# Sharing the normal forms of a LayerNorm between ScalarE and VectorE in an FFT mixer and MLP training step

## The chip, the cores and the metric

One core of a Trainium2 chip runs the whole step as one program. The metric is the device time of that program in microseconds (us); for the kernel before, it is the median of three runs. Engines are named as the profile names them: PE (TensorE's matmuls), PEld (its weight loads), DVE (VectorE), ACT (ScalarE), POOL (GpSimd) and SP (SyncE, which here only issues DMAs).

## The reference

The reference computes a forward pass and all gradients of two residual blocks over x of shape 2048 x 448 (bf16). Cut to what matters:

```python
def _layernorm(x, axis=-1, eps=1e-5):
    m = jnp.mean(x, axis=axis, keepdims=True)
    v = jnp.var(x, axis=axis, keepdims=True)
    return (x - m) / jnp.sqrt(v + eps)

def _A_ref(x, w_r, w_i):                   # spectral mixer
    X = jnp.fft.rfft2(x.astype(jnp.float32), axes=(-2, -1))
    y = jnp.fft.irfft2(X * (w_r + 1j * w_i), s=(S, D), axes=(-2, -1))
    return y.astype(jnp.bfloat16)

def _B_ref(x, w1, b1, w2, b2):             # token MLP, with a second layernorm inside
    u = gelu(jnp.einsum("bsd,sf->bdf", _layernorm(x), w1) + b1)
    return (jnp.einsum("bdf,fs->bds", u, w2) + b2).transpose(0, 2, 1)

h  = x + _A_ref(_layernorm(x), A_w_r, A_w_i)
h2 = h + _B_ref(_layernorm(h), B_w1, B_b1, B_w2, B_b2)
# outputs: h2 and the gradients of x, w_r, w_i, w1, b1, w2, b2 for a given grad_out
```

## The kernel before

The 2048 rows of x are held as 16 tiles of 128 partitions (row q * 16 + h in partition q of tile h), and the tiles are worked in four row groups g of four tiles. The stages around the change are these, in the order of the code.

**Statistics and normal forms** (class `Norm`). For each tile DVE computes bn_stats and bn_aggr (L279, L281). After the fourth tile of a group, `finish` runs: ACT takes the square root (L289), DVE the reciprocal and two small products (L290 to L293), and then ACT writes four normal forms, one per tile, as scale and bias from columns (L296). The class is used twice: for x (tiles `xln`) and later for h (tiles `hln`).

**Step 1 of the FFT** (`fft_rows`). For one row group DVE folds the normal forms into even and odd parts (`eo`, L303 to L305); PE runs 16 small matmuls into four PSUM tiles (L311); each PSUM tile is evicted into `zt` by ACT (L194) or DVE (L196), as a string of four letters says ("a" or "v"). In the forward pass it runs once per group right behind the statistics of that group.

**dg.** The product of grad_out and w2, needed much later, is cut into 14 pieces dg(j) of 16 matmuls (L438), each on one transposed tile of w2 (`w2T`, four buffers, loaded by DMA transposes on SP at L175). dg(0) to dg(3) stand behind step 1 in the code, each of dg(1) to dg(4) may start only behind the L311 matmuls of one row group (`folded[...][0]`), and the rest stand behind the whole spectral chain.

**The spectral chain.** `fft_cols` (step 2: L329 to L343, then output matmuls L321 to L323 with the table `hf`), the complex product `cmul` (L362 to L365), `ifft_cols` (L379 to L400), `ifft_rows` (L409 to L418), and for each of the 16 row tiles of the result the sum with x (L475) and h's statistics. The third part of the table `hf` is the negative of the second, made by DVE (L199, called at L458) behind a given instruction of group 3's step 1: `folded[3][1]`, the last instruction of the fold.

**The MLP.** 14 accumulations over the 16 `hln` tiles (L519, w1 in tiles `w1c` that take over the space of `zt` and others), gelu and its derivative, the second product (L587), then the backward pass, which calls `fft_rows`, `fft_cols` and the inverse steps once more with other tables.

The order of each engine's instructions is written when the program is built, by a scheduler that works with estimated durations and lets work that comes earlier in the code go first where several instructions could start. So PE's order is not the code's order: dg's matmuls appear in the trace between the steps of the spectral chain. Loads given to `nxt` are issued by SP in the order of the code, one behind the other. `issue_after` adds an order between two instructions of the same engine.

Of the kernel before, what the change touches and what calls it, by code (L numbers as in the profile page):

```python
# [13 lines left out]
ALU = mybir.AluOpType  # L14
ACT = mybir.ActivationFunctionType
# [98 lines left out]
def kernel(  # L114
# [21 lines left out]
    ve, ac, po, pe = nc.vector, nc.scalar, nc.gpsimd, nc.tensor  # L136
# [7 lines left out]
    def slot(i, shape, name):  # L144
        return big.tile(shape, BF16, tag=f"s{i}", name=name)
# [4 lines left out]
    def e4(shape, name):  # L150
        return ring.tile(shape, BF16, tag="e4", bufs=3, name=name)
# [7 lines left out]
    def col(n, name, dtype=F32):  # L159
        return ring.tile([P, n], dtype, tag=name, bufs=4, name=name)  # L160
# [4 lines left out]
    def ps_sp(shape, dtype=F32):  # L165
        return psum.tile(shape, dtype, tag="sp", bufs=5, name="ps_sp")
# [24 lines left out]

    def ev(out, in_, on):
        if on == "a":
            ac.copy(out=out, in_=in_)  # L194
        else:
            ve.tensor_copy(out=out, in_=in_)  # L196

    def neg(out, in_):
        ve.tensor_scalar(out=out, in0=in_, scalar1=-1.0, scalar2=None, op0=ALU.mult)  # L199
# [5 lines left out]
    x = slot(0, [P, NT, D], "x")  # L205
# [64 lines left out]
    class Norm:  # L270
# [14 lines left out]
        def finish(self, g):  # L285
            mv = self.mv[:, :].rearrange("p (i c) -> p i c", c=2)
            r = self.rstd[:, 4 * g:4 * g + 4]
            sq = col(4, f"sq_{self.nm}")
            ac.activation(out=sq[:], in_=mv[:, :, 1], func=ACT.Sqrt, bias=self.eps_col[:], scale=self.scale)  # L289
            ve.reciprocal(out=r, in_=sq[:])  # L290
            ve.tensor_scalar(out=self.rneg[:, 4 * g:4 * g + 4], in0=r, scalar1=self.back, scalar2=None, op0=ALU.mult)
            nb = col(4, f"nb_{self.nm}")
            ve.scalar_tensor_tensor(out=nb[:], in0=mv[:, :, 0], scalar=-1.0, in1=r, op0=ALU.mult, op1=ALU.mult)  # L293
            for i in range(4):
                h = 4 * g + i
                ac.activation(out=self.dst[:, h, :], in_=self.src[:, h, :], func=ACT.Identity,  # L296
                              scale=self.rstd[:, h:h + 1], bias=nb[:, i:i + 1])


    def fft_rows(src, zt, g, on, behind=None):  # L300
        eo = e4([P, 4, D], "eo")
        a, b = src[:, 4 * g:4 * g + 4, 1:224], src[:, 4 * g:4 * g + 4, 447:224:-1]
        ve.tensor_tensor(out=eo[:, :, 1:224], in0=a, in1=b, op=ALU.add)  # L303
        ve.tensor_tensor(out=eo[:, :, 225:448], in0=a, in1=b, op=ALU.subtract)
        fold = ve.tensor_copy(out=eo[:, :, 0:225:224], in_=src[:, 4 * g:4 * g + 4, 0:225:224])  # L305
        for i in range(4):
            h = 4 * g + i
            pz = ps_sp([P, 4, P])
            with tc.issue_after(behind.ins) if behind is not None else nullcontext():
                for c, o in enumerate((0, 97, 225, 320)):  # L310
                    last = pe.matmul(pz[:, c, :], lhsT=eo[:, i, o:o + P], rhs=kf[:], start=True, stop=True)  # L311
            ev(zt[:, :, :, 8 * h:8 * h + 8], pz[:, :, :].rearrange("p c (s k) -> p c s k", k=8), on[i])
        return last, fold

    def fft_cols(zt, dtab, dst):
        e_t = dtab[:, 0:2 * DF].rearrange("p (c k) -> p c k", c=2)
# [54 lines left out]
    def ifft_cols(ys, ab):  # L371
# [16 lines left out]
        for r in (1, 2, 3, 4, 5, 6, 7, 0, 8):  # L388
            p0 = half(r)
            if r in (0, 8):  # L390
                for kind in range(2):
                    ev(ab[:, kind, :, :, r, :], view(p0)[:, kind], "av"[kind])
                continue
            p1 = half(16 - r)
            t1 = f2([P, 2, 2, P], "t1")
            ac.copy(out=t1[:], in_=p1[:])
            st_ = 16 - 2 * r
            ve.tensor_tensor(out=ab[:, 0, :, :, r:17 - r:st_, :].rearrange("p c h k l -> p k c h l"),
                             in0=view(p0), in1=view(t1), op=ALU.add)
            ve.tensor_tensor(out=ab[:, 1, :, :, 16 - r:r - 1:-st_, :].rearrange(  # L400
                "p c h k l -> p k c h l"), in0=view(p0), in1=view(t1), op=ALU.subtract)
        return lasts[-1]

    def ifft_rows(ab, itab, h):
        a_t = itab[:, 0:2 * DF].rearrange("p (c k) -> p c k", c=2)
        b_t = itab[:, 2 * DF:4 * DF].rearrange("p (c k) -> p c k", c=2)
        pq = ps_sp([P, 2 * DF])
        for c in range(2):
            pe.matmul(pq[:, 0:DF], lhsT=ab[:, 0, c, h, :, :], rhs=a_t[:, c, :], start=(c == 0), stop=(c == 1))  # L409
        for c in range(2):  # L410
            pe.matmul(pq[:, DF:], lhsT=ab[:, 1, c, h, :, :], rhs=b_t[:, c, :], start=(c == 0), stop=(c == 1))  # L411
        eo = k1([P, 2 * DF], "eo2")
        ev(eo[:], pq[:], "a")
        py = ps_sp([P, D])
        pe.matmul(py[:, 0:DF], lhsT=kinv[:, 0, :], rhs=eo[:, 0:DF], start=True, stop=False)
        pe.matmul(py[:, DF:D], lhsT=kinv[:, 0, :], rhs=eo[:, 223:0:-1], start=False, stop=False)
        pe.matmul(py[:, 0:DF], lhsT=kinv[:, 1, :], rhs=eo[:, DF:2 * DF], start=False, stop=False)
        pe.matmul(py[:, DF:D], lhsT=kinv[:, 2, :], rhs=eo[:, DF + 223:DF:-1], start=False, stop=True)  # L418
        return py


    xln = slot(1, [P, NT, D], "xln")
    nx = Norm(x, xln, rstd_x, rneg_x, eps_x, 1.0, -1.0 / D, "x")
    zt = slot(2, [P, 4, NR, P], "zt")
    folded = []
    for g in range(4):
        for i in range(4):
            nx.stats(4 * g + i)
        folded.append(fft_rows(xln, zt, g, "avav" if g else "aava"))


    du = slot(7, [P, NFB, 450], "du")
# [148 lines left out]
    for t0 in range(0, NT, 4):  # L581
# [7 lines left out]
        for i in range(4):  # L589
# [3 lines left out]
                                    op0=ALU.add, op1=ALU.add)  # L593
# [32 lines left out]
    for h in range(NT):  # L626

        if h in (10, 14):
            fft_rows(dh, zt2, h // 4 - 2, "aava", w1_last)
        if h == 4:  # L630
            goT = slot(4, [P, 4, S], "goT")
            with tc.issue_after(w1T_last.ins):
                ld_t4(goT[:], grad_out[0])
        if h == 4:
            with tc.issue_after(w1T_last.ins):
                ld(df0[:], hnd["df0"].ap())
                ld(di1[:], hnd["di1"].ap())
        w1T = w4([P, NFB, P], "w1T")
        with tc.issue_after(chain[-1].ins):
            w1T_last = ld_t(w1T[:], w1Tv[h])  # L640
        pd = ps_mm([P, D + 1])
        for j in range(NFB):
            w1_last = pe.matmul(pd[:], lhsT=w1T[:, j, :], rhs=du[:, j, 0:D + 1], start=(j == 0), stop=(j == NFB - 1))  # L643
        norm_back(pd, True, hln[:, h, :], rstd_h[:, h:h + 1], rneg_h[:, h:h + 1], go_r[:, h, :], dh[:, h, :])


    with tc.issue_after(w1T_last.ins):
        load_w(w_b, lambda load, out, in_: load(out, in_))
    fft_rows(dh, zt2, 2, "aava")

    g_t = slot(0, [P, 4, F], "g_t")
# [119 lines left out]
```

## Time and profile before

| | |
|---|---|
| median of three runs | 372.22 us (370.95 to 372.51) |
| the profiled execution | 371.55 us |
| its span, first to last instruction | 369.8 us |
| granted TensorE clock | 1.00 |
| DMA over the span | 86.48 MB, mean 234 GB/s |

A page of the profile gives busy times per engine, the span in 40 slices, the DMA queues, the chain of work that ended last, and groups of like instructions. A timeline row reads: start, duration, engine, line, operation, tile written <- tiles read, shapes, count, and in brackets the idle time of the engine before it with what ended that. A group row reads: busy time, mean ns of one | idle time before and what ended it. A row of stretches gives, for each engine, busy us and the number of instructions, then the granted clock, the mean busy share of the DMA engines and GB/s.

### The profile page before, as it was taken

The numbers are of one execution on the slowest core, as the hardware profiler recorded it, in microseconds if no ns is written. First come the engines' busy times: TensorE is split into PE (matmuls) and PEld (weight loads), VectorE is DVE, ScalarE is ACT, GpSimd is POOL, SyncE is SP. The second block draws the span as 40 slices with busy tenths as digits, with TensorE's granted clock in tenths as the row PEclk, the third lists the DMA queues.
The fourth block names the chain that finished last, engine by engine and source line by source line (L and its number), as shares of the span: only waits on it lengthen the run. The fifth ranks groups of instructions, "written<-read, shape, count | busy, mean of one in ns | idle before, by whom it ended". The sixth has DMA issues, their size and how long they took to land.

```text
span 369.8 us, 5755 instructions
## 1 busy us (share of the span) xinstructions
PE 346.6 (94%) x2100; PEld 200.4 (54%) x2115; DVE 236.3 (64%) x557; ACT 217.4 (59%) x415; POOL 61.2 (17%) x107
## 2 busy tenths in 40 slices
PE   0698999999989999999999999999999999999996
PEld 0355667666645555555555555566655555665553
DVE  4873679967744999621167778468996566599000
ACT  2776555446659998109222234967656666777664
POOL 1000000001112211500540000101012522255311
PEclk9999999999999999999999999999999999999999
DMA  7999998997889999999998875791874444956633
GB/s 279 258 257 307 270 274 245 310 240 259 249 251 176 338 346 291 380 401 215 261 224 159 185 147 208 162 182 61 204 199 184 163 177 166 337 187 255 250 150 149
DMA packets 132524, 86.48 MB, mean 234 GB/s; under 512 B 91952, under 2 KB 123824, under 8 KB 131984
## 3 DMA queue, kind: packets, MB, share of 16 engines
q1 hardware_dynamic: 124304, 55.78, 61.2%
q0 software_dynamic: 8048, 30.31, 22.3%
q8 instruction: 16, 0.26, 0.3%
q14 instruction: 12, 0.10, 0.1%
q10 hardware_dynamic: 144, 0.03, 0.0%
HBM read 32.81 MB, written 30.76 MB: 172 GB/s over the span
## 4 chain that ended last, share of the span: by engine, by line
PE 65%; DVE 17%; ACT 8%; DMA 4%; SPq 3%; issue 2%; ACTq 0%; DVEq 0%
PE ps_mm L732 12%; PE ps_mm L662 10%; PE ps_sp L587 7%; PE ps_mm L438 6%; PE ps_mm L519 6%; PE ps_sp L519 5%; PE ps_mm L587 4%; DMA w2T<-in_B_w_dram 4%; DVE junk L615 3%; DVE junk L617 3%; ACT v L610 3%; SPq L175 2%; DVE t_r L362 2%; DVE gg L349 2%; DVE t_i L363 2%
## 5 line engine op out<-in xcount | busy, mean ns | idle before, releaser
L194 ACT CAST s<-ps_mm 128x512 bf16<-128x512 f32 (+1 forms) x107 | 57.5, 557 | 25.6 <-PE ps_mm L662 11.1
L662 PE MATMUL ps_mm<-goT,g_t 128*128 128x512 bf16 x214 | 53.3, 379 | 2.0 <-ACT s L194 1.5
L438 PE MATMUL ps_mm<-go_nat,w2T 128*128 128x448 bf16 x224 | 50.5, 357 | 1.0 <-DMA w2T<-in_B_w_dram 1.0
L732 PE MATMUL ps_mm<-du_t,hlnT 128*128 128x512 bf16 (+1 forms) x251 | 49.3, 352 | 0.3
L643 PE MATMUL ps_mm<-du,w1T 128*128 128x449 bf16 x224 | 43.4, 353 | 0.0
L732 PEld LDWEIGHTS <-hlnT 128*128 128x128 bf16 x256 | 25.1, 98 | 22.2
L587 PE MATMUL ps_sp<-gT,w2c 128*128 128x448 bf16 x140 | 35.6, 352 | 0.0
L610 ACT ACTIVATE v<-ps_mm,nm,rstd_h 128x448 f32<-128x448 f32 x16 | 11.6, 723 | 39.2 <-DVE nm L608 39.2
L172 POOL DMA_DIRECT2D out_dram<-s x29 | 15.6, 539 | 112.4 <-ACT s L194 86.3
L519 PEld LDWEIGHTS <-w1c 128*128 128x128 bf16 x224 | 21.8, 98 | 20.7 <-issue 1.9
L587 PEld LDWEIGHTS <-w2c 128*128 128x128 bf16 x224 | 21.9, 98 | 20.5
L643 PEld LDWEIGHTS <-w1T 128*128 128x128 bf16 x224 | 21.7, 97 | 20.7
L662 PEld LDWEIGHTS <-g_t 128*128 128x128 bf16 x224 | 21.6, 97 | 20.7 <-issue 1.4
L438 PEld LDWEIGHTS <-w2T 128*128 128x128 bf16 x224 | 21.9, 99 | 16.2 <-DMA w2T<-in_B_w_dram 1.9
L349 DVE TENSOR_TENSOR gg<-ps_sp,gi 128x450 bf16<-128x450 f32 x28 | 16.2, 621 | 17.0 <-ACT gi L346 17.0
L587 PE MATMUL ps_mm<-gT,w2c 128*128 128x448 bf16 x84 | 25.0, 352 | 0.0
L519 PE MATMUL ps_mm<-hln,w1c 128*128 128x448 bf16 x112 | 24.4, 352 | 0.5 <-DVE b1col L508 0.2
L194 ACT CAST eo<-ps_sp 128x450 bf16<-128x450 f32 x32 | 17.2, 538 | 12.5 <-PE ps_sp L411 12.2
L519 PE MATMUL ps_sp<-hln,w1c 128*128 128x448 bf16 x112 | 23.1, 352 | 0.0
L311 PE MATMUL ps_sp<-kf,eo 128*128 128x128 bf16 x128 | 9.3, 231 | 14.0 <-DVE eo L305 14.0
L592 DVE SCALAR_TENSOR_TENSOR h<-ps_sp,b2col,hr 128x448 bf16<-128x448 f32 x10 | 6.3, 679 | 25.1 <-PE ps_sp L587 25.1
L615 DVE CUSTOM_DVE_ANT_0 junk<-ps_sp,xr,rneg_x 128x448 bf16<-128x448 f32 x16 | 10.9, 683 | 16.3 <-ACT v L612 16.3
(146 smaller groups left out, 625.9 us busy)
## 6 DMA issues: line engine op xcount, KB each, us to landing
w1c<-in_B_w_dram SPq DMA_DIRECT2D x7, 1024.0 KB, 7.4
w2c<-in_B_w_dram SPq DMA_DIRECT2D x8, 896.0 KB, 12.6
out_dram<-s POOLq DMA_DIRECT2D x14, 512.0 KB, 2.9
out_dram<-s POOLq DMA_DIRECT2D x15, 448.0 KB, 2.9
xs_d<-xs SPq DMA_DIRECT2D x1, 1800.0 KB, 7.7
xs_b<-xs_d SPq DMA_DIRECT2D x1, 1800.0 KB, 8.9
x<-in_A_x_dram SPq DMA_DIRECT2D x4, 448.0 KB, 4.3
go_nat<-in_grad_out_dram SPq DMA_DIRECT2D x2, 896.0 KB, 7.5
```

Of the source, the lines that this page charges most:

```text
L172: return (eng or po).dma_start(out=out, in_=in_)
L194: ac.copy(out=out, in_=in_)
L349: ve.tensor_tensor(out=gg[:], in0=pr[:], in1=gi[:], op=op)
L438: pe.matmul(pg[:], lhsT=w2T[j][:, t, :], rhs=go_nat[:, t, :], start=(t == 0), stop=(t == NT - 1))
L519: pe.matmul(pu[:], lhsT=wc[:, h, o:o + P], rhs=hln[:, h, :], start=(h == 0), stop=(h == NT - 1))
L587: pe.matmul(p2[i][:], lhsT=w2c[t0 // 4][:, j, i * P:(i + 1) * P], rhs=gT[:, j, :], start=(j == 0), stop=(j == NFB - 1))
L610: ac.activation(out=v[:], in_=ps[:, 0:D], func=ACT.Identity, scale=rstd_c, bias=nm1[:])
L615: ve.tensor_tensor_reduce(out=junk[:], in0=ps[:, 0:D], in1=xhat, scale=rneg_c, scalar=0.0, op0=ALU.mult, op1=ALU.add, accum_out=nm2[:])
L617: ve.scalar_tensor_tensor(out=junk[:], in0=xhat, scalar=nm2[:], in1=v[:], op0=ALU.mult, op1=ALU.add)
L643: w1_last = pe.matmul(pd[:], lhsT=w1T[:, j, :], rhs=du[:, j, 0:D + 1], start=(j == 0), stop=(j == NFB - 1))
L662: mm = pe.matmul(pw[:], lhsT=g_t[:, c, j * P:(j + 1) * P], rhs=goT[:, c, 512 * n:512 * n + 512], start=(c == 0), stop=(c == 3))
L732: pe.matmul(pw[:, 0:wdt], lhsT=hlnT[:, c, h * P:(h + 1) * P], rhs=du_t[:, c, 512 * n:512 * n + wdt], start=(c == 0), stop=(c == 3))
```

## The change

Three things are changed. In `finish`, two of the four normal forms of a group (i = 2 and 3) are made by DVE as one tensor_scalar with two column operands, for all four groups of x and for the last group of h; the others stay on ACT. In x's step 1 the evictions of groups 0 to 2 all go to ACT ("aaaa"), while group 3 keeps "avav"; before, it was "aava" for group 0 and "avav" for the others. And `fft_rows` returns its last eviction in place of the last instruction of the fold, so that hf's negative stands behind the last eviction of group 3, which is DVE's.

```diff
     def ev(out, in_, on):
         if on == "a":
-            ac.copy(out=out, in_=in_)
-        else:
-            ve.tensor_copy(out=out, in_=in_)
+            return ac.copy(out=out, in_=in_)
+        return ve.tensor_copy(out=out, in_=in_)
...
             for i in range(4):
                 h = 4 * g + i
-                ac.activation(out=self.dst[:, h, :], in_=self.src[:, h, :], func=ACT.Identity,
-                              scale=self.rstd[:, h:h + 1], bias=nb[:, i:i + 1])
+
+                if i > 1 and (self.nm == "x" or g == 3):
+                    ve.tensor_scalar(out=self.dst[:, h, :], in0=self.src[:, h, :], scalar1=self.rstd[:, h:h + 1],
+                                     scalar2=nb[:, i:i + 1], op0=ALU.mult, op1=ALU.add)
+                else:
+                    ac.activation(out=self.dst[:, h, :], in_=self.src[:, h, :], func=ACT.Identity,
+                                  scale=self.rstd[:, h:h + 1], bias=nb[:, i:i + 1])
...
-        fold = ve.tensor_copy(out=eo[:, :, 0:225:224], in_=src[:, 4 * g:4 * g + 4, 0:225:224])
+        ve.tensor_copy(out=eo[:, :, 0:225:224], in_=src[:, 4 * g:4 * g + 4, 0:225:224])
...
-            ev(zt[:, :, :, 8 * h:8 * h + 8], pz[:, :, :].rearrange("p c (s k) -> p c s k", k=8), on[i])
-        return last, fold
+            done = ev(zt[:, :, :, 8 * h:8 * h + 8], pz[:, :, :].rearrange("p c (s k) -> p c s k", k=8), on[i])
+        return last, done
...
-        folded.append(fft_rows(xln, zt, g, "avav" if g else "aava"))
+        folded.append(fft_rows(xln, zt, g, "avav" if g == 3 else "aaaa"))
```

## Prediction, made before the changed kernel was run

> **What bounds the kernel now.** I read the page's engine shares and slices first, to see which engine sets the time.
>
> ```profile
> PE 346.6 (94%) x2100; PEld 200.4 (54%) x2115; DVE 236.3 (64%) x557; ACT 217.4 (59%) x415; POOL 61.2 (17%) x107
> PE   0698999999989999999999999999999999999996
> ```
>
> PE is busy for 346.6 of 369.8 us, so 23.2 us are all that can be won without removing matmuls, and this change removes none. The edit acts on DVE and ACT; what counts is which PE gaps close. Hence the second view, the PE timeline of x's row groups.
>
> ```profile
> 12.43 1.89 PE L311 MATMUL ps_sp<-kf,eo 128*128 128x128 bf16 x16 [12.43 <-DVE eo L305]
> 14.11 3.99 PE L438 MATMUL ps_mm<-go_nat,w2T 128*128 128x448 bf16 x16
> 18.43 1.12 PE L438 MATMUL ps_mm<-go_nat,w2T 128*128 128x448 bf16 x5 [0.33 <-DMA w2T<-in_B_w_dram]
> 19.38 1.06 PE L311 MATMUL ps_sp<-kf,eo 128*128 128x128 bf16 x16
> 26.49 3.19 PE L438 MATMUL ps_mm<-go_nat,w2T 128*128 128x448 bf16 x16
> 31.04 1.07 PE L311 MATMUL ps_sp<-kf,eo 128*128 128x128 bf16 x16 [1.36 <-DVE eo L305]
> 31.94 1.30 PE L438 MATMUL ps_mm<-go_nat,w2T 128*128 128x448 bf16 x6
> ```
>
> Gaps: 12.43 us before group 0's step-1 matmuls (L311), 0.33 us for the second w2T, and 1.36 us before group 3's, where dg(3) ended at 29.68 and dg(4) may not come before that L311. From 31.94 on, the dg matmuls (L438) are filler between the steps of the spectral chain, and the third view shows where that filler meets its data: the queue of SP and each transfer's way to its landing.
>
> ```profile
> 11.97 11.19 SPq L175 DMA_TRANSPOSE w2T<-in_B_w_dram  x4
> ...
> 24.77 0.43 SPq L169 DMA_DIRECT2D w_t<-in_A_w_i_dram  x1
> 25.30 9.79 SPq L175 DMA_TRANSPOSE w2T<-in_B_w_dram  x1
> ...
> L175 SPq DMA_TRANSPOSE w2T<-in_B_w_dram x1: 3833/3833/3833, 12.0 to 12.0; - x1
> DMA to landing us min/median/max: 6.4/6.4/6.4
> ...
> L175 SPq DMA_TRANSPOSE w2T<-in_B_w_dram x1: 9787/9787/9787, 25.3 to 25.3; - x1
> DMA to landing us min/median/max: 11.9/11.9/11.9
> ...
> 5.00:38.00 33.00, 23.84 (x170) 14.59 (x171) 21.45 (x65) 21.21 (x39) 0.00 (x0) 1.00 1.08 285
> ```
>
> SP issues back to back and the DMA share from 5 to 38 us is 1.08 (last but one column): these landings come from the DMA engines, not from compute. The second w2T lands at 12.0 + 6.4 = 18.4, the sixth at 25.3 + 11.9 = 37.2 us. Who needs the sixth?
>
> ```profile
> 33.48 0.92 PE L438 MATMUL ps_mm<-go_nat,w2T 128*128 128x448 bf16 x4
> 35.04 0.92 PE L438 MATMUL ps_mm<-go_nat,w2T 128*128 128x448 bf16 x4
> 37.03 1.49 PE L438 MATMUL ps_mm<-go_nat,w2T 128*128 128x448 bf16 x7
> ```
>
> dg(4) has 16 matmuls: 6 + 4 + 4, and two of these seven. Three more take 1.49 - 0.92 = 0.57 us, so one takes 0.19, and the first one of dg(5) starts at 37.03 + 2 x 0.19 = 37.4, only 0.2 us behind the landing. Whatever PE wins before 37 us runs into that transfer. That is the crux.
>
> **The change part by part.** Durations are from groups of instructions and the ACT and DVE timelines:
>
> ```profile
> L525 DVE TENSOR_SCALAR zz<-zz x5: 269/271/276, 115.0 to 146.4; 128x448 bf16<-128x448 bf16 x5
> L617 DVE SCALAR_TENSOR_TENSOR junk<-hln,nm,v 128x448 bf16<-128x448 bf16 x16 | 11.0, 685 | 0.6
> 8.37 2.71 ACT L296 ACTIVATE xln<-x,nb_x,rstd_x 128x448 bf16<-128x448 bf16 x4 [0.52 <-DVE nb_x L293]
> 13.07 1.07 ACT L194 CAST zt<-ps_sp 128x512 bf16<-128x512 f32 x2 [0.23 <-PE ps_sp L311]
> L196 DVE CAST zt<-ps_sp 128x512 bf16<-128x512 f32 x7 | 4.5, 687 | 1.1 <-PE ps_sp L311 1.0
> 11.11 0.63 DVE L303 TENSOR_TENSOR eo<-xln 128x892 bf16<-128x892 bf16 x1 [0.24 <-ACT xln L296]
> 14.83 1.15 DVE L279 BATCH_NORM_STATS2 bs_x<-x 128x6 f32<-128x448 bf16 x2 [0.21 <-DMA x<-in_A_x_dram]
> 30.88 0.69 DVE L199 TENSOR_SCALAR hf<-hf 128x2048 bf16<-128x2048 bf16 x1
> 34.55 0.26 PE L323 MATMUL ps_sp<-gg,hf 128*128 128x225 bf16 x1
> ```
>
> A normal form on ACT takes 2.71/4 = 0.68 us in a row. On DVE the new tensor_scalar reads scale and bias from columns, which no 448-wide row shows; the bounds are 0.27 (constants, same shape) and 0.69 (column scalar and a second tensor, L617). I take 0.3, since it has one tensor as L525 has. Eight in x cost DVE 2.4 us, at most 5.5. DVE's zt evictions fall from 7 to 2: 5 x 0.69 = 3.4 us less. So DVE is between 1.0 us relieved and 2.1 us burdened. ACT loses 8 x 0.68 = 5.4 and gains 5 x 0.54 = 2.7 us.
>
> Start: two forms on ACT end 2 x 0.68 = 1.36 us sooner; the two on DVE run from 8.4 to 9.0, beside ACT's. The fold (L303 to L305) then starts at about 9.9 instead of 11.11, group 0's matmuls at 11.2, dg(0) at 12.9 and ends at 16.9. dg(1) still cannot start before 18.4, but group 1's L311 now fits into that hole: ACT has four evictions and two forms ahead of its fold, 4 x 0.54 + 2 x 0.68 = 3.5 us from 11.9 on, so 15.4; DVE may by then be in the statistics of x's third load (14.83), one or two of 0.6 us; the fold itself takes 1.3 (11.11 to 12.43). That makes 16.7 to 17.9, and the hole ends at 18.4, so most of the 0.9 us lies in it; I count all.
>
> From 18.43 PE went without a gap to 29.68 with 48 dg matmuls and two L311 groups. With one group (0.9 us) gone, dg(3) ends at 28.8. Group 3's fold must be done then, not at 31.0: on ACT each of groups 2 and 3 spends two forms less (-1.36) and two evictions more (+1.07), 0.6 us less for both, and the run up to them starts some 1.9 us sooner (group 1's L311 at 17.5, not 19.38), which puts the fold of group 3 at 31.0 - 0.6 - 1.9 = 28.5. The gap of 1.36 closes, and dg(4) starts at 28.8 + 0.9 = 29.7, which is 2.2 us sooner than 31.94. At 0.69 per form each group's pair takes 0.8 us longer on DVE; if that falls wholly on group 3's fold, dg(4) comes 1.4 us sooner.
>
> The negative of hf moves behind DVE's last eviction. The evictions follow L311 at 28.8 and take DVE to about 30.6, so it runs to 31.3; its first reader is L323, at 34.55 before and 2.2 sooner, 32.3, after. What it moves past are the two evictions, which no longer stand behind its 0.69 us. I cost it at nothing, since 1 us of PE's filler and chain work covers it; without that cover it would cost up to 0.7. Returning the instruction from the eviction issues nothing.
>
> Then the sixth w2T, for which two rows of a round of the chain are needed:
>
> ```profile
> 37.23 0.54 ACT L346 COPY gi<-ps_sp 128x450 f32<-128x450 f32 x1 [0.24 <-PE ps_sp L343]
> L349 DVE TENSOR_TENSOR gg<-ps_sp,gi 128x450 bf16<-128x450 f32 x28 | 16.2, 621 | 17.0 <-ACT gi L346 17.0
> ```
>
> From dg(4)'s start to dg(5)'s there were 37.41 - 31.94 = 5.5 us of PE work, so PE would ask at 35.2 for what lands at 37.2. Of the 2.2 us the old slack keeps 0.2; 2.0 stand against the wait. The rest depends on what lies ahead of dg(5) in PE's order, which is not the code's order but the scheduler's. The spectral chain stands earlier in the code than this filler; if its estimates see the late landing, it puts chain work there. A round without filler stands through a copy (0.54) and an add (0.62) on other engines, 1.2 of the 2.0 us, so I count 0.8 filled. Kept: 1.0 us.
>
> Next is a PE gap behind the chain:
>
> ```profile
> 75.74 0.36 PE L438 MATMUL ps_mm<-go_nat,w2T 128*128 128x448 bf16 x1 [0.71 <-DMA w2T<-in_B_w_dram]
> SPq L169 <- PE ps_sp L343: 2.1, 1, 2.1
> 57.02 2.55 SPq L169 DMA_DIRECT2D w1c<-in_B_w_dram  x2
> ```
>
> This w2T stands on SP behind w1c, and w1c waited 2.1 us for the chain to release zt (L343). A chain up to 2 us ahead moves that queue as far, and the wait of 0.71 goes: 0.7 us.
>
> h's last group shows little to win:
>
> ```profile
> 101.43 3.13 PE L519 MATMUL ps_mm<-hln,w1c 128*128 128x448 bf16 x13
> 106.41 3.19 PE L519 MATMUL ps_sp<-hln,w1c 128*128 128x448 bf16 x16
> 109.77 0.35 PE L519 MATMUL ps_mm<-hln,w1c 128*128 128x448 bf16 x1 [0.17 <-ACT hln L296]
> 108.96 2.71 ACT L296 ACTIVATE hln<-x,nb_h,rstd_h 128x448 bf16<-128x448 bf16 x4 [0.51 <-DVE nb_h L293]
> ```
>
> PE waits 0.17 us for the first form, which stays on ACT, and then works two accumulations in turn while the others appear. The two DVE forms come 1.4 us sooner but nobody waits: 0 to 0.2, counted at 0.
>
> Sum: 0.2 + 0.8 + 0.7 = 1.7 us. The profiled execution, 371.55 us (1.75 around its span), would become 369.85; from the runs' median of 372.22 I get 370.5.
>
> **The rivals.** *All is lost at the sixth w2T.* The order ahead of dg(5) stays as it is and PE waits 2.0 us there. For it: at 18.43 and at 75.74 PE stood waiting for a w2T, so the order had been made in the belief that both would land sooner. Then only 0.2 us stay: 372.0.
>
> *All is kept.* If PE has chain work enough ahead of dg(5), or if the transfer lands sooner, 2.2 + 0.7 + 0.2 = 3.1 us: 369.1. Against it: SP's queue had no pause up to 25.3 that earlier compute could shorten. [...]
>
> *Slower: the cover of h's tail is spent early.* After the last ifft_rows, PE runs 3.19 us of a second accumulation (106.41) while h's last statistics and forms are made. If the new order, made from other estimates, puts these 16 matmuls ahead of the last rows as it does with 13 others at 101.43, PE stands idle from 106.4 to 109.6. It decides once more than half of them are gone (1.6 us), about what the change gains. With the gain lost as in the first rival: 372.0 + 3.0 = 375.0. For it: PE's order follows estimates, and the chain shifts against the filler. Against: the edit touches only the last group's forms there, 1.4 us of ACT, and nothing ahead of the last rows.
>
> **How the numbers follow.** Forecast 0.44, all lost 0.22, all kept 0.17, slower 0.17. The forecast's own range is 369.5 (1.6 of the 2.0 us filled and h's 0.2: 2.7 us won) to 371.3 (none filled, the wait at 75.74 gone: 0.9). The 0.69 us form lies in it: dg(4) 1.4 sooner, 0.2 + 0.4 x 1.2 + 0.7 = 1.4 us. Half a per cent, about what a measurement here can tell from no change, is 1.86 us: below 370.36 lie all of "kept" and nearly half of the forecast (0.21): 0.38. Above 374.08 lies the slower rival: 0.17. Same: 0.45. The range from 368.6 to 373.9 leaves out the slower rival and the lower edge of "kept", about 0.2.
>
> **What would show it.** Right, step by step: the first L311 near 11.2 us, group 1's L311 ahead of dg(1), no gap before group 3's, a new DVE row of about 0.3 us x10, dg(4) near 29.7; then a wait for w2T on PE near 36 to 37 us of about 1.2 us, w1c issued near 55, and no wait at dg(11). A wait of 2 us at the sixth w2T and the same times from 37.4 on would be the first rival. The forecast is wrong if DVE's forms take 0.6 us or more, if group 3's gap stays, or if PE's gaps after 93 us grow past 1.2 us.

## The result, and the profile after

The changed kernel takes 369.59 us in the median (368.86 to 370.40, 6 runs), the kernel before 372.45 us on the same chip (370.95 to 373.69, 6 runs): 2.86 us less, a ratio of 0.9934 with an interval of 0.9916 to 0.9952. The profiled execution took 368.86 us, its span 367.1 us. In the kernel after, the lines from `fft_rows` on carry numbers 4 higher (L311 is L315, L438 is L442, L519 is L523).

The page of the kernel after, its PE row and its slices:

```profile
PE 347.4 (95%) x2115; PEld 200.4 (55%) x2115; DVE 236.7 (64%) x562; ACT 213.8 (58%) x410; POOL 61.3 (17%) x107
PE   0898999999999999999999999999989999999996
```

PE's work is the same (346.6 us before, where 15 matmul records are missing from the trace), and the span is 2.7 us shorter: PE stood idle less. The second of its slices of 9 us went from 6 tenths to 8. The PE timeline of x's row groups in the kernel after:

```profile
10.43 1.89 PE L315 MATMUL ps_sp<-kf,eo 128*128 128x128 bf16 x16 [10.43 <-DVE eo L309]
16.59 1.07 PE L315 MATMUL ps_sp<-kf,eo 128*128 128x128 bf16 x16 [0.55 <-DVE eo L309]
28.16 1.07 PE L315 MATMUL ps_sp<-kf,eo 128*128 128x128 bf16 x16 [0.35 <-DVE eo L309]
29.06 1.30 PE L442 MATMUL ps_mm<-go_nat,w2T 128*128 128x448 bf16 x6
36.24 0.55 PE L442 MATMUL ps_mm<-go_nat,w2T 128*128 128x448 bf16 x2 [0.98 <-DMA w2T<-in_B_w_dram]
```

The first step-1 matmuls come 2.0 us sooner, group 1's stand ahead of the second w2T, group 3's gap is down from 1.36 to 0.35 us. The first three of the six matmuls at 29.06 still belong to dg(3), so dg(4) starts at 29.06 + 3 x 0.19 = 29.63 (31.94 before). dg(5) then waits 0.98 us for the sixth w2T.

PE's work is fixed, so the end is the first start plus the work plus all waits. The waits of PE between 13 and 113 us, first of the kernel before, then of the kernel after (columns: us in total, times, longest):

```profile
PE ps_sp L311 <- DVE eo L305: 1.4, 1, 1.4
PE ps_mm L438 <- DMA w2T<-in_B_w_dram: 1.0, 2, 0.7
PE ps_sp L415 <- ACT eo L194: 0.7, 1, 0.7
```

```profile
PE ps_sp L315 <- DVE eo L309: 1.3, 3, 0.6
PE ps_mm L442 <- DMA w2T<-in_B_w_dram: 1.0, 1, 1.0
PE ps_sp L419 <- ACT eo L194: 0.3, 1, 0.3
```

Up to the end of dg(13) the waits have only changed places: 1.36 + 0.33 + 0.71 = 2.40 us before, 0.55 + 0.38 + 0.35 + 0.98 = 2.26 after. The rest of the gain there is the start: 12.43 - 10.43 = 2.0, in all 2.14. The first matmuls of the MLP show it, and the two rows after them the tail (of each pair the first row is of the kernel before):

```profile
93.63 2.27 PE L519 MATMUL ps_mm<-hln,w1c 128*128 128x448 bf16 x11 [0.24 <-DVE b1col L508]
106.02 0.26 PE L415 MATMUL ps_sp<-eo,kinv 128*128 128x225 bf16 x1 [0.68 <-ACT eo L194]
```

```profile
91.49 1.67 PE L523 MATMUL ps_mm<-hln,w1c 128*128 128x448 bf16 x8 [0.24 <-DVE b1col L512]
103.23 0.26 PE L419 MATMUL ps_sp<-eo,kinv 128*128 128x225 bf16 x1 [0.30 <-ACT eo L194]
106.98 0.35 PE L523 MATMUL ps_mm<-hln,w1c 128*128 128x448 bf16 x1 [0.17 <-ACT hln L300]
```

93.63 - 91.49 = 2.14 us; 106.02 - 103.23 = 2.79 us. Of the 0.65 us between the two, 0.38 is the shorter wait for the last `eo`, and the rest are gaps too short to be listed. From there on nothing changes: h's first form was 2.79 us sooner, the end of the span 2.7.

One part of this is not the change's. The first statistics begin when x lands (kernel before, then after):

```profile
4.96 1.16 DVE L279 BATCH_NORM_STATS2 bs_x<-x 128x6 f32<-128x448 bf16 x2 [4.02 <-DMA x<-in_A_x_dram]
```

```profile
4.28 1.15 DVE L278 BATCH_NORM_STATS2 bs_x<-x 128x6 f32<-128x448 bf16 x2 [3.34 <-DMA x<-in_A_x_dram]
7.67 0.70 DVE L297 TENSOR_SCALAR xln<-x,rstd_x,nb_x 128x448 bf16<-128x448 bf16 x2
```

and the group of the new forms (busy us, mean ns of one | idle before):

```profile
L297 DVE TENSOR_SCALAR xln<-x,rstd_x,nb_x 128x448 bf16<-128x448 bf16 x8 | 2.8, 391 | 0.1
```

x landed 0.68 us sooner in the second profile, so the change itself moved the start by 1.3 us. The new DVE form takes 391 ns, a pair of them 0.70 us.

So far this reads as "PE starts sooner". The experiments show that this alone is not worth 2.9 us. What decides is an order. The program's list of PE instructions, counted (S: a row group's 16 step-1 matmuls, F: dg matmuls, b, U: the MLP's, y and q: ifft_rows):

```
before: S F21 S F27 S F16 S F6 ... F1 b2 U11 ... U13 y4 q4 y4    U188
after:  S F15 S F27 S F19 S F6 ... F4 b2 U8  ... U14 y4 q4 U2 y4 U188
```

Ahead of group 3's step 1 stand 21 + 27 + 16 = 64 dg matmuls before, all of dg(0) to dg(3), and 61 after. The scheduler's estimates saw group 3's fold ready sooner, it seems, and it put step 1 three matmuls sooner. From there on the pattern of chain and filler (dg's matmuls between the steps of the chain) is the same up to the chain's ifft_cols (59 us before, 57 us after), so through all of it the spectral chain has done the same work with three filler matmuls (0.57 us) fewer ahead of it: a lead. Near the end, two U matmuls stand ahead of the last ifft_rows step (y4), and they cover part of the wait for `eo`, 0.30 us instead of 0.68.

### The profile page after: what moved, and what is told of

It is laid out like the page before. It is cut to its first block, busy times and chain, and to the rows that moved or that the text cites. A ratio compares the mean times of both kernels' runs of the same rounds, so it can differ in the third digit from the quotient of the medians.

```text
span 367.1 us, 5776 instructions
## 1 busy us (share of the span) xinstructions
PE 347.4 (95%) x2115; PEld 200.4 (55%) x2115; DVE 236.7 (64%) x562; ACT 213.8 (58%) x410; POOL 61.3 (17%) x107
## 4 chain that ended last, share of the span: by engine, by line
PE 64%; DVE 20%; ACT 9%; DMA 4%; issue 2%; ACTq 0%; DVEq 0%
PE ps_mm L736 12%; PE ps_mm L666 10%; PE ps_sp L591 7%; PE ps_mm L523 6%; PE ps_sp L523 5%; PE ps_mm L442 5%; PE ps_mm L591 4%; DMA w2T<-in_B_w_dram 3%; DVE junk L619 3%; DVE junk L621 3%; ACT v L614 3%; DVE t_r L366 2%; DVE gg L353 2%; PE ps_sp L415 2%; DVE t_i L367 2%
## 5 line engine op out<-in xcount | busy, mean ns | idle before, releaser
L666 PE MATMUL ps_mm<-goT,g_t 128*128 128x512 bf16 x224 | 55.2, 379 | 1.6 <-ACT s L194 1.5
L442 PE MATMUL ps_mm<-go_nat,w2T 128*128 128x448 bf16 x224 | 50.3, 356 | 1.0 <-DMA w2T<-in_B_w_dram 1.0
L591 PEld LDWEIGHTS <-w2c 128*128 128x128 bf16 x224 | 21.9, 98 | 20.5
L523 PEld LDWEIGHTS <-w1c 128*128 128x128 bf16 x224 | 21.8, 98 | 20.1 <-issue 1.3
L442 PEld LDWEIGHTS <-w2T 128*128 128x128 bf16 x224 | 21.7, 98 | 16.1 <-DMA w2T<-in_B_w_dram 1.7
L523 PE MATMUL ps_mm<-hln,w1c 128*128 128x448 bf16 x112 | 23.8, 352 | 0.4 <-DVE b1col L512 0.2
L523 PE MATMUL ps_sp<-hln,w1c 128*128 128x448 bf16 x112 | 22.6, 352 | 0.0
L315 PE MATMUL ps_sp<-kf,eo 128*128 128x128 bf16 x128 | 9.3, 231 | 11.9 <-DVE eo L309 11.9
```

What stands on the lines that cost most here:

```text
L442: pe.matmul(pg[:], lhsT=w2T[j][:, t, :], rhs=go_nat[:, t, :], start=(t == 0), stop=(t == NT - 1))
L523: pe.matmul(pu[:], lhsT=wc[:, h, o:o + P], rhs=hln[:, h, :], start=(h == 0), stop=(h == NT - 1))
L591: pe.matmul(p2[i][:], lhsT=w2c[t0 // 4][:, j, i * P:(i + 1) * P], rhs=gT[:, j, :], start=(j == 0), stop=(j == NFB - 1))
L666: mm = pe.matmul(pw[:], lhsT=g_t[:, c, j * P:(j + 1) * P], rhs=goT[:, c, 512 * n:512 * n + 512], start=(c == 0), stop=(c == 3))
```

## The experiments

Two theories were set against each other: PE's early start in x's row groups less what the sixth w2T takes back (the prediction's; A in the texts of the runs, later E), and the lead (L), which arose from the fourth run. Each kernel was timed beside the kernel before.

| run | median us (range) | ratio to before (interval) |
|---|---|---|
| forms in x alone, on the kernel before | 370.42 (369.26-373.38) | 0.9965 (0.9937-0.9993) |
| evictions alone, on the kernel before | 372.98 (371.83-374.86) | 1.0025 (1.0001-1.0049) |
| h's last group alone, on the kernel before | 371.53 (370.70-372.63) | 0.9990 (0.9971-1.0009) |
| the change without h's part | 369.70 (369.28-370.64) | 0.9939 (0.9917-0.9962) |
| the change, w_t behind the sixth w2T | 368.83 (368.37-370.06) | 0.9905 (0.9884-0.9926) |
| before, w_t behind the sixth w2T | 372.21 (371.38-374.30) | 0.9995 (0.9978-1.0012) |
| before, with the lead alone | 370.92 (369.68-372.99) | 0.9970 (0.9951-0.9990) |
| as the fifth, the stores of `xln` moved too | 369.81 (368.24-373.87) | 0.9940 (0.9913-0.9968) |
| the change again | 369.59 (369.05-370.42) | 0.9936 (0.9914-0.9958) |
| the change without the lead | 371.12 (370.63-372.95) | 0.9979 (0.9960-0.9997) |
| the change, negative behind the fold | 370.27 (369.88-371.05) | 0.9953 (0.9936-0.9970) |
| the fifth with a lead of six | 368.95 (368.58-369.97) | 0.9920 (0.9898-0.9941) |

The kernel before had medians of 371.83 us beside the first four, 372.23 beside the next four and 371.89 beside the last four.

**One part at a time.** The forms in x alone:

```diff
+                if i > 1 and self.nm == "x":
+                    ve.tensor_scalar(...)
```

> The kernel before with one part alone: DVE makes two of four forms in x's groups; evictions, h and hf's negative as before. Theory A (the forms carry the gain): first L311 about 1.3 us sooner than before for the same landing of x, group 3's L311 three dg matmuls ahead of dg(3)'s end, a wait of 1 to 2 us at the sixth w2T, and 2.0 to 2.8 us of the 2.86 us of the whole change: 369.7 to 370.5. Theory B (the forms alone overload DVE, which still has 7 zt evictions, and only together with the evictions do they pay): group 3's gap of about 1 us stays and the time is 371.3 or more.

Measured: 370.42 us, 1.4 less. The time lies in theory A's range, but the gain is short of the 2.0 to 2.8 us that it asked for, and there is no wait at the sixth w2T. Its order has the same lead of three as the change. But its runs fall into two groups, eight from 369.26 to 371.07 and four from 372.25 to 373.38; in the last four the granted clock over the span is 0.995, in the others 0.998 to 1.0. The profiled run is one of the four; four rows of its timeline and clock follow. DVE and PE:

```profile
31.26 0.69 DVE L199 TENSOR_SCALAR hf<-hf 128x2048 bf16<-128x2048 bf16 x1 [3.33 <-DMA hf<-tab_hf]
31.87 1.28 DVE L196 CAST zt<-ps_sp 128x512 bf16<-128x512 f32 x2
33.25 0.36 PE L334 MATMUL ps_sp<-df,zt 128*128 128x225 bf16 x2 [3.06 <-issue]
```

and of the stretch behind (start:end, length, busy us of PE, PEld, DVE, ACT and POOL, clock, DMA share, GB/s):

```profile
33.80:37.20 3.40, 3.40 (x14) 1.80 (x12) 0.00 (x0) 1.55 (x3) 0.00 (x0) 0.50 0.71 149
```

This chain is worth reading slowly. Here hf's negative still stands behind the fold, ahead of DVE's two evictions of group 3. With the forms shared, DVE gets to it early, and hf has not landed: DVE stands 3.33 us, the evictions behind it too, and PE's first matmul on `zt` waits 3.06 us. The row says "issue", because the profile saw no releaser; the DVE rows name it. Behind the gap the clock is at 0.50 for 3.4 us (last row).

The evictions alone:

```diff
-        folded.append(fft_rows(xln, zt, g, "avav" if g else "aava"))
+        folded.append(fft_rows(xln, zt, g, "avav" if g == 3 else "aaaa"))
```

> The kernel before with one part alone: groups 0 to 2 evict on ACT only. Theory A: ACT now has four evictions and four forms per group, 2.1 + 2.7 us, so the folds of groups 1 to 3 come 0.5 to 1 us later and PE's gap before group 3's L311 grows from 1.4 to about 2.4 us; slower by 0 to 1 us: 372.4 to 373.4. Theory B (DVE is what delays the folds): faster by 1 us or more, 371.4 or less.

372.98 us, 1.2 more than before, as expected by theory A. ACT here has the added evictions and still all the forms, and group 3's gap grows from 1.36 us:

```profile
32.20 1.07 PE L311 MATMUL ps_sp<-kf,eo 128*128 128x128 bf16 x16 [2.02 <-DVE eo L305]
```

h's last group alone, and the change without it:

```diff
+                if i > 1 and self.nm == "h" and g == 3:      # alone, on the kernel before
...
-                if i > 1 and (self.nm == "x" or g == 3):     # the change without it
+                if i > 1 and self.nm == "x":
```

> The kernel before with one part alone: DVE makes two of four forms of h's last group. Theory A (nobody waits for them): 372.3, between 0 and 0.2 us faster, and PE's waits at the end of h (0.68 for the eviction of the last ifft_rows, 0.17 for the first form) stay. Rival (the part of the gain that shows behind 93 us, 0.65 us, comes from here): 371.8, with the wait of 0.68 us shortened.

> The changed kernel without its h part: all of h's forms on ACT. Theory A: as the changed kernel, 369.6 to 369.8, with PE's wait at the last ifft_rows still 0.3 us. Rival (h's part gives what shows behind 93 us): 370.2, with that wait back at 0.7 us.

371.53 beside 371.83, and 369.70 beside the change's 369.59: h's part does nothing measurable. The second of these profiles says more. In it the sixth w2T landed late, at 37.6:

```profile
37.67 0.55 PE L442 MATMUL ps_mm<-go_nat,w2T 128*128 128x448 bf16 x2 [2.03 <-DMA w2T<-in_B_w_dram]
```

PE waited 2.03 us and came to dg(5) 0.26 us later than the kernel before (37.41). By the first rival nothing is then left of the gain. The span is 368.4 us all the same, 1.4 less than the 369.8 of before. So something gains behind 37 us, and that is where the theory of the lead came from.

**The sixth w2T.** SP issues w_t's two loads just ahead of it, and w_t's first reader starts only at 41.0 us in the change (DVE, L366). Moved behind it:

```diff
-    load_w(w_t, nxt)
     for j in range(1, 4):
         dg(j)
+        if j == 1:
+            load_w(w_t, nxt)
```

> The changed kernel with one load order changed: the two loads of w_t (1.8 MB) go to SP behind the sixth w2T instead of ahead of it. Theory A (PE's wait of 1 to 2 us at the sixth w2T is what the change loses): the sixth w2T lands at about 31 us, the wait is gone, dg(5) starts near 35.3 us, and the time falls by 0.8 to 1.5 us, held back by the ninth w2T, which left 0.8 us of slack: 368.2 to 368.9. Rival (a later limit takes it back anyway, so the wait costs nothing): 369.6.

> The kernel before with the same load order. Theory A: PE never waited there (0.2 to 0.3 us of slack), so nothing changes: 371.6 to 372.0. Rival (the load order helps by itself, wherever the forms are made): 371.0 or less.

On the change: 368.83 us, 0.76 less than the change by the medians, the lowest median of this study; the two intervals overlap, so the size is uncertain. SP was through with the sixth w2T at 30.2 us (its row: 23.76, 6.43 long), dg(5) started at 35.7, and the view of PE's waits from 13 to 113 us holds no w2T at all:

```profile
PE ps_sp L315 <- DVE eo L309: 1.0, 3, 0.4
PE ps_sp L325 <- DVE gg L353: 0.3, 2, 0.2
PE ps_sp L419 <- ACT eo L194: 0.3, 1, 0.3
PE ps_mm L524 <- DVE b1col L513: 0.2, 1, 0.2
PE ps_mm L524 <- ACT hln L300: 0.2, 1, 0.2
```

On the kernel before the same edit does nothing (372.21), as expected: there dg(5) had 0.2 us of slack. So the wait of 1 us in the change costs about 0.8 us.

**The lead.** On the kernel before, with forms, evictions and negative untouched, the last three matmuls of dg(3) were ordered behind group 3's step 1:

```diff
-        with tc.issue_after(folded[min(j - 1, 3)][0].ins) if j else nullcontext():
-            for t in range(NT):
+        for t in range(NT):
+            behind = folded[3] if j == 3 and t >= NT - 3 else folded[min(j - 1, 3)]
+            with tc.issue_after(behind[0].ins) if j else nullcontext():
```

> The kernel before with the last three matmuls of dg(3) ordered behind group 3's step-1 matmuls, as the scheduler places them in the changed kernel, so that the spectral chain runs three filler matmuls (0.57 us) ahead of its old place; nothing starts earlier. Theory L (the lead is worth something by itself): PE's gap before group 3 grows by 0.57 us, but the wait for the twelfth w2T (0.7 to 1.2 us) shrinks by about that and the wait at the last ifft_rows goes from 0.7 to 0.3 us: 371.0 to 371.8. Rival (only the earlier start counts): slower by 0.6, 372.4.

370.92 us, 1.3 less than before, although this makes PE idle longer ahead of group 3:

```profile
31.22 1.75 PE L311 MATMUL ps_sp<-kf,eo 128*128 128x128 bf16 x16 [1.95 <-DVE eo L305]
```

```profile
31.40:34.80 3.40, 3.40 (x22) 2.27 (x20) 1.73 (x3) 1.70 (x3) 0.00 (x0) 0.50 1.18 203
```

(The stretch behind shows the clock at 0.50 again. The profiled run, 372.99 us, and three more of the twelve, 371.97 to 372.38, have a mean clock of 0.994 to 0.995; the other eight, 0.998 to 1.0, lie from 369.68 to 371.30.) The row of dg(11), which waits for the twelfth w2T, and SP's row of `w1c`, which comes ahead of that transfer, will be needed below:

```profile
58.87 2.25 SPq L169 DMA_DIRECT2D w1c<-in_B_w_dram  x2
78.61 0.55 PE L439 MATMUL ps_mm<-go_nat,w2T 128*128 128x448 bf16 x2 [0.38 <-DMA w2T<-in_B_w_dram]
```

The counter-test takes the lead out of the change and leaves all the rest:

```diff
-        folded.append(fft_rows(xln, zt, g, "avav" if g == 3 else "aaaa"))
+        if g < 3:
+            folded.append(fft_rows(xln, zt, g, "aaaa"))
...
     for j in range(1, 4):
-        dg(j)
+        mm = dg(j)
+    folded.append(fft_rows(xln, zt, 3, "avav", behind=mm))   # step 1 behind dg(3)'s last matmul
```

> The changed kernel itself, beside the next three. Both theories: 369.3 to 369.9 us, ratio to the kernel before 0.992 to 0.994.

> The changed kernel with group 3's step-1 matmuls ordered behind the last matmul of dg(3), as in the kernel before, instead of three matmuls sooner; every evictor, form and load as changed. Theory L (the chain's lead of three filler matmuls carries the gain behind 36 us): the wait for the twelfth w2T of some 0.7 us and the tail's 0.7 us come back, and 1.0 to 1.6 us are lost against the changed kernel: 370.5 to 371.2. Theory E (PE simply starts sooner, and what is left of that after the sixth w2T carries the gain): 369.3 to 369.9, as the changed kernel; group 3's gap of 0.35 us would close, so rather a little less.

371.12 us against 369.59: 1.5 us lost, and no run of the one kernel overlaps with the other's. Against the kernel before (371.89) 0.8 us are left: that is what the rest of the change is worth without the lead. PE's waits from 13 to 113 us without the lead:

```profile
PE ps_mm L443 <- DMA w2T<-in_B_w_dram: 3.4, 3, 1.7
PE ps_sp L419 <- ACT eo L194: 0.7, 1, 0.7
```

and a row of its SP queue and one of its PE timeline:

```profile
56.54 2.39 SPq L169 DMA_DIRECT2D w1c<-in_B_w_dram  x2
```

```profile
76.06 0.36 PE L443 MATMUL ps_mm<-go_nat,w2T 128*128 128x448 bf16 x1 [1.52 <-DMA w2T<-in_B_w_dram]
```

The start is as early as in the change (10.67 us), dg(4) comes at 29.75, and yet the waits for w2T come to 3.4 us in this profile. Of these, 1.65 us at the sixth w2T lie within the 1.0 to 2.0 us that the profiles of the change and of the change without h's part show there. The wait of 1.52 us at dg(11) shows what the lead does. The transfer for dg(11) stands on SP behind w1c, and w1c is released by the chain. Without the lead PE asks for it at 76.06 - 1.52 = 74.54, that is 18.0 us after w1c's issue at 56.54; before, 75.03 - 57.02 = 18.0 too. In the change:

```profile
55.18 2.38 SPq L169 DMA_DIRECT2D w1c<-in_B_w_dram  x2
```

```profile
74.00 0.92 PE L442 MATMUL ps_mm<-go_nat,w2T 128*128 128x448 bf16 x4
```

dg(11) is the third of these four. Two matmuls take 0.55 us in a row, so PE asks for its transfer at 74.00 + 0.55 = 74.55, 19.4 us after w1c. With the lead alone it is 78.61 - 0.38 - 58.87 = 19.4 too. By the order of the instructions, one more step of ifft_rows (four y and four q, from 73.22 to 74.00 in the change, 0.78 us) stands ahead of dg(11) with the lead, and three filler matmuls (0.57 us) fewer ahead of w1c's release: 1.35 us more for the transfer (19.4 - 18.0 = 1.4 by the times). The transfer landed 18.9 us after w1c in the change, 18.7 before and 19.5 without the lead; over all profiles that wait for it, 18.6 to 20.5. All five profiles without the lead wait at dg(11), 0.65 to 1.52 us; of the eight with a lead of three, three do, 0.38 to 1.12 us. At the last dg matmul both orders have done the same work, so the lead costs nothing there. And the wait for the last `eo` is 0.7 us in each of the five profiles without the lead and 0.3 in each of the eight with a lead of three (0 with a lead of six).

**The negative.** The change, with the negative behind the fold as it was:

```diff
-        ve.tensor_copy(out=eo[:, :, 0:225:224], in_=src[:, 4 * g:4 * g + 4, 0:225:224])
+        fold = ve.tensor_copy(out=eo[:, :, 0:225:224], in_=src[:, 4 * g:4 * g + 4, 0:225:224])
...
-        return last, done
+        return last, fold
```

> The changed kernel with hf's negative behind group 3's fold again, ahead of DVE's two evictions of group 3 (0.69 us). The prediction costed this part at nothing: 369.3 to 369.9, as the changed kernel. Rival: the evictions come 0.7 us later and the chain's first step waits for them: up to 370.4.

370.27 us against 369.59, 0.7 more. The two intervals overlap, so the size is uncertain; the mechanism stands in the rows, and it is that of the first run:

```profile
30.18 0.69 DVE L198 TENSOR_SCALAR hf<-hf 128x2048 bf16<-128x2048 bf16 x1 [1.89 <-DMA hf<-tab_hf]
30.79 1.28 DVE L195 CAST zt<-ps_sp 128x512 bf16<-128x512 f32 x2
32.17 0.36 PE L333 MATMUL ps_sp<-df,zt 128*128 128x225 bf16 x2 [1.62 <-issue]
```

Part of the 1.62 us is paid back: PE comes to the sixth w2T later and does not wait there in this profile, where the change waits 0.98 us. In the change, the order of the same DVE instructions is the other way round, and nothing waits for hf:

```profile
28.82 1.29 DVE L195 CAST zt<-ps_sp 128x512 bf16<-128x512 f32 x2 [0.72 <-PE ps_sp L315]
30.02 0.68 DVE L198 TENSOR_SCALAR hf<-hf 128x2048 bf16<-128x2048 bf16 x1
30.21 0.36 PE L333 MATMUL ps_sp<-df,zt 128*128 128x225 bf16 x2
```

**Further.** Two attempts to go below 368.8. The first also moved the stores of `xln` behind later w2T loads:

```diff
-    for g in range(4):
-        nxt(ld, xln_d[:, 4 * g:4 * g + 4, :], xln[:, 4 * g:4 * g + 4, :])
...
+        if j == 5:
+            for g in range(4):
+                nxt(ld, xln_d[:, 4 * g:4 * g + 4, :], xln[:, 4 * g:4 * g + 4, :])
```

> The changed kernel with the load order of the sixth w2T and, further on, with the four stores of xln behind the ninth and tenth w2T instead of ahead of them. Theory A: the ninth w2T lands several us sooner as well, so its slack of 0.8 us no longer holds PE back, and the time is 368.0 to 368.5, up to 0.5 us below the kernel with the first reordering alone. Rival (compute holds the rest): the same as with the first reordering alone.

369.81 us (368.24 to 373.87): no gain, the expectation missed. In its profile SP starts the ninth w2T at 42.57 us instead of the 46.91 of the fifth run's, but PE waits 1.12 us for the twelfth. Three of its runs show a mean clock of 0.994 to 0.995; why is open. The second was a lead of six:

> The changed kernel with w_t's loads behind the sixth w2T, and a lead of six filler matmuls instead of three (the last six of dg(3) behind group 3's step-1 matmuls). Theory L: the waits that the lead closes are down to 0.3 us at the tail, and PE's gap ahead of group 3 grows by 0.57 us: 368.7 to 369.3 against 368.8 with three, the lead is used up. A theory by which every matmul of lead is worth 0.4 us (1.3 us for three): 367.6.

368.95 us, as with three (368.83) and as theory L expected: a gain with every further matmul, 367.6, is ruled out. The last wait for `eo` is gone, 0.30 us less, and the gap ahead of group 3 has grown from 0.35 us by the time of three matmuls:

```profile
28.30 1.07 PE L315 MATMUL ps_sp<-kf,eo 128*128 128x128 bf16 x16 [0.91 <-DVE eo L309]
```

## Why the prediction was right, and where it was not

370.5 us was forecast, 1.7 less than before; it became 2.86 less. The direction and the range held, two of the steps did not hold, and one reason was wrong. That the sum came near is in part luck: one kept microsecond hung on the landing of one transfer, another term came true for another reason, and the negative and the tail, both put at nothing, were worth about 0.7 us each.

- *The start and the row groups*: right. The first L311 1.2 us sooner by the working, 1.3 measured once x's landing is taken out; group 1's step 1 in the hole before the second w2T; dg(4) 2.2 sooner by the working, 2.3 measured. Part of that is x's landing again: in two other profiles of the old order (h's last group alone, and before with w_t moved), where x landed at 4.3 to 4.4 us, dg(4) started at 31.48 and 31.72, that is 1.9 and 2.1 us later than in the change. The form was taken at 0.3 us and took 0.39, 0.31 behind the first. The gap of group 3, named as a sign of being wrong if it stays, did not close wholly: 0.35 us stayed, because three filler matmuls fewer stand ahead of it; without the lead it is closed. Groups 1 and 2 got gaps of 0.55 and 0.38 us that the working did not foresee.
- *"0.8 filled" at the sixth w2T*: failed. The scheduler put no chain work ahead of dg(5); the order there is as before. The profile after kept 37.41 - 36.24 = 1.2 us, about the forecast's 1.0, but only because this transfer landed at 36.2 instead of 37.2. In other profiles of the change's order it landed at 36.7 and 37.6. The wait costs about 0.8 us (fifth run). That SP's queue left no room for an earlier landing was true of the compute, not of the order of its loads: with w_t behind it, SP was through with the transfer at 30.2 instead of 34.1 (24.48 + 9.60 in the change), and PE did not wait for it.
- *The negative at nothing*: failed; moving it was worth about 0.7 us by the medians (370.27 against 369.59). The prediction named the 0.69 us of DVE work and its cover, and did not ask what the instruction itself waits for. The row was there, in the answer on hf in the kernel before:

```profile
L169 SPq DMA_DIRECT2D hf<-tab_hf x1: 432/432/432, 23.8 to 23.8; - x1
DMA to landing us min/median/max: 5.9/5.9/5.9
```

  23.8 + 5.9 = 29.7 us, and the negative ran at 30.88: 1.2 us of slack. Group 3's step 1 came 2.9 us sooner (31.04 to 28.16), more than that slack, and with the negative still ahead of the evictions PE paid.
- *The wait at dg(11) goes, 0.7 us*: the wait went, for another reason. "A chain up to 2 us ahead moves that queue as far" is true (w1c was issued at 55.18 instead of 57.02), but the matmul that asks moves with it: without the lead the asking stayed 18.0 us behind w1c's issue, and the wait grew to 1.5. It went because the order gave the transfer 1.35 us more.
- *h's part at nothing*: right in size. *The tail*: the prediction had its mechanism, PE's work beside the last ifft_rows, only as the slower rival. It came with the opposite sign: two U matmuls moved in ahead of the last step, and PE's wait for h's first form stayed at 0.17. With the short gaps beside it that gave 0.65 us that no term held.
- *The first rival* (all lost at the sixth w2T, 372.0) is refuted by the profile in which all was lost there and the span was 1.4 us shorter. *The second* (all kept, 369.1) came near by its time, but not by its mechanism; where that wait is really gone, the time is 368.8.
- *The DMA share*: the prediction took the share of 1.08, beside 285 GB/s from 5 to 38 us, as a sign that the landings come from the DMA engines. The profile of the lead alone moved 406 GB/s at a share of 0.99 from 30 to 31.4 us, the kernel before 391 GB/s at 0.95. So a share of about 1 beside 285 GB/s did not mean that 285 was the limit.

## What to carry to other kernels

When the same engine runs a critical chain and filler, ask not only when each starts but which is ahead of which: here three filler matmuls put behind one chain step were worth 1.3 to 1.5 us, though they made nothing start sooner. A chain and the consumer of its late transfer that moved together gained nothing at that wait: without the lead the asking stayed 18.0 us behind w1c's issue, and the wait went from 0.71 to 1.52 us. Before an instruction is costed at nothing, read what it waits for as well as what it delays: here a DVE operation of 0.69 us, which waited 1.89 us in one run and 3.33 us in another for a DMA, held back the two evictions queued behind it, and PE stood 1.62 and 3.06 us.

## What the runs showed of the hardware

- In two profiles the clock fell behind a short gap of PE. In the kernel before with the lead alone it was 0.50 for 3.4 us behind a gap of 1.95 us, with the forms in x alone behind one of 3.06 us; behind gaps of 2.02 us (the evictions alone) and 2.03 us (the change without h's part) it stayed at 1.00, and the mean of both profiled runs is 1.0. That the gap is the cause is read from the order in time; no run varied the gap alone. In each of these first two kernels four of twelve runs have a mean clock of 0.994 to 0.995, which is what 3.4 us at half the clock make of some 370 us, and their medians lie 2.7 us (forms in x) and 1.7 us (the lead) above those of the other eight.
- The same transfer lands up to 1.4 us apart in executions of the same order (the sixth w2T: 36.2, 36.7 and 37.6 us), and x's first tiles 0.7 us apart. Beside that the 0.2 us of slack ahead of dg(5) in the kernel before are little, and the 0.98 us that PE waits for this transfer in the one profile of the change are uncertain by as much.
